# A fused attention and two-MLP kernel on Trainium2: where in a step GpSimd issues its half of the relayout

## The chip, the cores and the metric

The kernel runs on 1 core of one Trainium2 chip. The metric is the device time of one execution in microseconds; the kernel before was run three times: 644.7, 645.08 and 647.82 us, median 645.08 us.

## The reference, cut to what matters

Attention with two mixings of the heads (one before and one behind the softmax), followed by two MLPs. Batch 2, 12 heads, 448 positions, head width 64; 896 tokens of width 768; both MLPs have 2048 hidden units. Everything is float32.

```python
scores = scale * np.matmul(q, k.transpose(0, 1, 3, 2))
scores = np.einsum('bhij,hg->bgij', scores, w_pre)
scores = scores - np.max(scores, axis=-1, keepdims=True)
attn = np.exp(scores)
attn = attn / (np.sum(attn, axis=-1, keepdims=True) + 1e-09)
attn = np.einsum('bhij,hg->bgij', attn, w_post)
return np.matmul(attn, v).astype(np.float32)
...
x = attn_out.transpose(0, 2, 1, 3).reshape(B * S, H * D)
x = elu(x @ moe_w_in) @ moe_w_out
return silu(x @ moe2_w_in) @ moe2_w_out
```

## The kernel before, in words

**Attention** (about the first third of the span). The scores come out of TensorE with query positions on the partitions: `qk_pair` (line 149) makes them for a tile T of 128 query rows and a pair of heads, and ScalarE and VectorE copy them to the SBUF tile `s` (`smap[T]`, lines 156 and 158). The mixing over heads needs heads on the partitions. So the **relayout**, a DMA from SBUF to SBUF, brings the scores of 10 query positions with all 12 heads, 120 rows of 448 floats, into the buffer `blk` (`move`, line 168). There are 45 such blocks for each batch, 90 in all.

The work goes on in **45 steps of two blocks each**, c = 0 and c = 1. `blk` has 3 slots (`NBUF`), and step s uses slot s % 3. In `step(s)`:

- `premix(s)` (line 198) multiplies both blocks by w_pre on TensorE: 8 matmuls, first the four of c = 0, then the four of c = 1.
- In steps 8, 10, 12 and so on, `av_pair` (line 269, 32 matmuls) multiplies finished attention rows by v. In steps 0 to 6, 11 to 16 and 17 to 34 `qk_pair` makes new scores (8 matmuls a step).
- `postmix(s - 1)` (line 241, 56 matmuls) applies w_post to the block pair of the step before.
- `rmax(s)` (VectorE, line 204), `exps(s)` (ScalarE, line 216, with the sums) and `recip(s)` make the softmax. `recip` has two small VectorE instructions (lines 224 and 225) and then two GpSimd instructions (line 229) that multiply w_post by 1/sum: this is the **softmax factor** `krn`, which `postmix(s)` reads in the next step.
- ScalarE and VectorE empty the PSUM banks: `qk_evac` (lines 156, 158), `post_evac` (lines 133, 135), `av_evac` (line 280). In a step without `av_pair`, `recip(s)` stands behind these in the program.
- `relayout(s + AHEAD)` with `AHEAD = 2` issues the DMAs for two steps later, and `run(D_AT, s)` issues loads from HBM.

The order is written out by hand, and each engine takes its instructions in the program's order; semaphores let an engine wait for another. A relayout into slot (s + 2) % 3 needs the slot that `premix(s - 1)` reads, and the rows of `smap` that it copies.

**Queues.** The relayout of c = 0, with the pieces that `early` puts a step ahead, goes through SP's queue, which also carries most loads from HBM. For steps 3 to 31 (`POOLED = (3, 32)`) the relayout of c = 1 is issued by GpSimd: 35 DMAs for 29 blocks, since some blocks come in two or three pieces. The relayouts for steps 0 to 2 and from step 32 on are on SP for both c. On GpSimd in a step stand, in this order: the two `krn` instructions of step s, the DMA for c = 1 of step s + 2, and in some later steps (from step 30 on) parts of the conversion of x for the first MLP (`split_x`, lines 391 and 392).

**The MLPs** (from about 206 us to the end) are rows of matmuls with weights that are loaded and split in time. The change does not touch them.

Of the kernel before, what the change touches and what calls it, by code (L numbers as in the profile page):

```python
# [18 lines left out]
B, H, S, D = 2, 12, 448, 64  # L19
# [11 lines left out]
NBUF = 3  # L31
NE = 3
LEAD = 5
POOLED = (3, 32)
# [3 lines left out]
AHEAD = 2  # L38
# [41 lines left out]
def attn_moe_moe(ctx: ExitStack, tc: tile.TileContext, q, k, v, w_pre, w_post, w1i, w1o, w2i, w2o, out):  # L80
    nc = tc.nc
# [24 lines left out]
    blkb = ap_.tile([P, NBUF, 2, S], F32, name="blk")  # L106
# [30 lines left out]
    smap = {}  # L137
# [14 lines left out]
    def qk_evac(e):  # L152
        for T, p, pq in sev:
            o = smap[T][:, 2 * p + e]
            if e == 0:
                nc.scalar.activation(o, pq[0], AF.Copy, scale=0.125)  # L156
            else:
                nc.vector.tensor_scalar(o, pq[1], 0.125, None, op0=ALU.mult)
        if e == 1:
            sev.clear()  # L160

    seq = [(b, n) for b in range(B) for n in range(KB)]
    NB = len(seq) // 2

    def move(s, c, piece):
        T, r, d, m, i = piece
        eng = nc.gpsimd if c and POOLED[0] <= s < POOLED[1] else nc.sync
        eng.dma_start(blkb[4 + H * i:4 + H * (i + m), s % NBUF, c], smap[T][r:r + d * (m - 1) + 1:d])

    def early(n):  # L170
        x = BLOCKS[seq[n]]
        return [y for y in x if n % 2 == 0 and y[0] < x[-1][0]]

    def relayout(s):

        if s >= NB:
            return
        for c in range(2):
            gone = early(2 * s + c)
            for piece in BLOCKS[seq[2 * s + c]]:  # L180
                if piece not in gone:
                    move(s, c, piece)
        if s + 1 < NB:
            for piece in early(2 * s + 2):
                move(s + 1, 0, piece)

# [5 lines left out]
    def premix(s):  # L192
        tags = (("pre1", "pre2"), ("av", "pre0"), ("qk1", "pre0"))[s % 2 + (s % 2 and s > NB - 9)]
        pre[s] = [ps.tile([P, S], F32, name=f"pre{s}_{r}", tag=tags[r], bufs=1) for r in range(2)]
        for c in range(2):
            for r in range(2):
                o = slice(HS * r, HS * r + (HS if r == 0 else BW))
                nc.tensor.matmul(pre[s][r][HS * c:HS * c + HS], kpre[o], blkb[o, s % NBUF, c], start=True, stop=True, tile_position=(HS * r, HS * c))  # L198

    def rmax(s):  # L200
        n = prow(s)
        nmx[s] = ap_.tile([P, 2], F32, name=f"nmx{s}", tag="nmx", bufs=3)
        for r in range(2):
            nc.vector.tensor_reduce(nmx[s][:n, r:r + 1], pre[s][r][:n], axis=AX.X, op=ALU.max, negate=True)  # L204
            if r == 0 and s - 1 in LATE:
                recip(s - 1)

    def exps(s, between=None):
        n = prow(s)
        pexp[s] = []  # L210
        sums[s] = ap_.tile([P, 2], F32, name=f"sum{s}", tag="sum", bufs=3)
        for r in range(2):
            if r and between:
                between()
            t = ap_.tile([P, S], F32, name=f"pe{s}_{r}", tag="pe", bufs=4)
            nc.scalar.activation(t[:n], pre[s][r][:n], AF.Exp, bias=nmx[s][:n, r:r + 1], scale=1.0, accum_out=sums[s][:n, r:r + 1])  # L216
            pexp[s].append(t)
        del pre[s], nmx[s]

    def recip(s):  # L220

        n = prow(s)
        z = sums.pop(s)
        nc.vector.tensor_scalar(z[:n], z[:n], 1e-9, None, op0=ALU.add)
        nc.vector.reciprocal(z[:n], z[:n])  # L225
        kr[s] = []
        for r in range(2):
            t = ap_.tile([P, H, 5], F32, name=f"krn{s}_{r}", tag="krn", bufs=4)
            nc.gpsimd.tensor_scalar(t[:n], kps[:n], z[:n, r:r + 1], None, op0=ALU.mult)  # L229
            kr[s].append(t)  # L230
# [3 lines left out]
    def postmix(s):  # L234

        w = pst[s] = [x.rearrange("p (r c) -> p r c", r=2) for x in pbank]
        for r, m in [(0, m) for m in range(6)] + [(0, 6), (1, 6)] + [(1, m) for m in range(6)]:
            u, j = r if m == 6 else m % 2, m // 2
            for c in range(2):
                o = slice(HS * c, HS * c + BW)  # L240
                nc.tensor.matmul(w[c][HS * u:HS * u + HS, r, j * BW:(j + 1) * BW], pexp[s][r][o, m * HS:(m + 1) * HS], kr[s][r][o].rearrange("p h i -> p (h i)"), start=True, stop=True, tile_position=(HS * c, HS * u))  # L241
        del pexp[s], kr[s]
# [4 lines left out]
    def post_evac(s):  # L247
        for c, w in enumerate(pst.pop(s)):
            b, n = seq[2 * s + c]
            T, n = 4 * b + n // 12, n % 12  # L250
            if T not in amap:
                amap[T] = ap_.tile([P, 4 * H, TI], F32, name=f"a{T}", tag="a", bufs=2)
            o = amap[T][:NV, :, n * BI:(n + 1) * BI].rearrange("p x (r i) -> p r x i", r=2)
            evac((nc.scalar, nc.vector)[c], o, w[:NV].rearrange("p r (x i) -> p r x i", i=5))
# [18 lines left out]
    def av_evac():  # L273
        for T, p, m, av in xev:
            b, t = tiles[T]
            if b not in xmap:
                xmap[b] = cp.tile([P, NP, S], F32, name=f"xr{b}", tag=f"xr{b}")
                if b == 1:
                    cp.tile([P, 40], F32, name="align3")
            nc.scalar.copy(xmap[b][:, p:p + 2, t * TI:t * TI + m], av[:, :, :m])  # L280
        xev.clear()

    def av_split():
        for T, p, m, av in xsp:
            c = slice(tiles[T][1] * TI, tiles[T][1] * TI + m)
            x = x1_tile()
            nc.scalar.copy(x[:, p:p + 2, 0, c], av[:, :, :m])
            nc.scalar.copy(xmap[1][:, p:p + 2, c], av[:, :, :m])
            nc.vector.tensor_tensor(x[:, p:p + 2, 1, c], av[:, :, :m], x[:, p:p + 2, 0, c], op=ALU.subtract)
        xsp.clear()  # L290
# [24 lines left out]
    for s in range(AHEAD):  # L315
        relayout(s)
# [8 lines left out]
    def at(d, step, f):  # L325
        d.setdefault(int(step), []).append(f)
# [20 lines left out]
    def run(d, s):  # L347
        for f in d.get(s, []):
            f()

    def step(s):
        if s < NB:
            premix(s)
        if s - 1 in LATE:
            rmax(s)
        run(X_AT, s)
        run(QK_AT, s)
        run(F_AT, s)
        if 0 <= s - 1 < NB:
            postmix(s - 1)  # L360
        if s < NB:
            if s - 1 not in LATE:
                rmax(s)
            exps(s, (lambda: post_evac(s - 1)) if s in TURN else None)
        two = s in X_AT
        if two:
            run(B_AT, s)
            if s < NB:
                recip(s)
            av_evac()  # L370
            av_split()
            run(A_AT, s)
        qk_evac(0)
        qk_evac(1)
        if 0 <= s - 1 < NB and s not in TURN:
            post_evac(s - 1)
        if not two:
            run(B_AT, s)
            if s < NB and s not in LATE:
                recip(s)  # L380
        relayout(s + AHEAD)
        run(D_AT, s)
        run(M_AT, s)
# [63 lines left out]
    def ring(n):  # L447
        if n >= O2:
            n += 2 * sum(x[0] == "out" and x[3][0] == KS and i % 2 == 1 for i, x in enumerate(chunks[O2:n]))
        return n % (NE + 1)  # L450
# [169 lines left out]
    for s in range(NB + 1):  # L620
        step(s)
        if s == NB - 2:
            cm_s2.__exit__(None, None, None)
            cm_s1.__exit__(None, None, None)
            cm_ws, mo["ws"] = pool("wst", bufs=1, side="right")
            load_w(NE)
            load_w(NE + 1)
# [369 lines left out]
    for t, n_ in zip(x, "B11_0 B11_1 B11_2 T1_0 T1_1 T1_2 B21_0 B21_1 B22_0 T2_0 T2_1 B22_1 T3_0 T3_1 T4_0 T4_1 B21_2 T2_2 T3_2 T4_2 B22_2".split()):  # L997
        a, i = n_.split("_")
        xt[1][a, int(i)] = t
    for n in range(O1 + 8, I2):  # L1000
# [4 lines left out]
        if po:  # L1005
            c = chunks[n][2]
# [122 lines left out]
    while n < NCH:  # L1129
        c, k = chunks[n][2:]  # L1130
# [4 lines left out]
        i = n - O2  # L1135
        xs = made[i] if i < len(made) else []
        nx = [x[3][0] == KS for x in chunks[n + 1:n + 3]]
        d = [(ring(n + 1) + i) % 4 for i in range(4)]
# [87 lines left out]
```

## Time and profile before

| | |
|---|---|
| three runs, median | 645.08 us (644.7 to 647.82) |
| profiled execution, its own time | 647.85 us |
| its span, from the first to the last instruction | 646.0 us |
| TensorE busy | 612.0 us (95%) |
| VectorE busy | 453.6 us (70%) |
| ScalarE busy | 374.0 us (58%) |
| GpSimd busy | 83.4 us (13%) |
| mean granted TensorE clock | 0.984 |
| chain that ended last, by share | TensorE 79%, DMA 9%, VectorE 4%, ScalarE 3%, GpSimd 2% |

The profile shows one execution. An engine is busy while it executes; waiting on semaphores and issuing DMAs on SP's or ScalarE's queue do not count. "PE" is TensorE's matmuls, "PEld" its weight loads, "DVE" VectorE, "ACT" ScalarE, "POOL" GpSimd, "SP" the queue engine. The chain of waits is found by going back from the last instruction, at each step to what released it. Within a window, the chain is the one that ended last in that window.

### The profile page before, as it was taken

To read this page: it belongs to the slowest core of one execution; us is meant where nothing else is said; L and a number is where in the kernel's file an instruction comes from. 1 tells how busy PE (TensorE), PEld (TensorE's weight loads), DVE (VectorE), ACT (ScalarE), POOL (GpSimd) and SP (SyncE) were. 2 spreads that over 40 slices of the span, in tenths; PEclk is the share of its full clock that TensorE was granted. 3 is DMA by queue.
4 is the path that set the end of the run, shared out by engine and by line. 5 is a ranking of instruction groups with operands and counts; after the bars stand their busy time and mean duration, and the time that the engine had idled before them with its cause. 6 is when DMAs were issued, how large, how long until landed. Compare 5 with 4: busy or idle time off the path is not lost.

```text
span 646.0 us, 15007 instructions
## 1 busy us (share of the span) xinstructions
PE 612.0 (95%) x6139; PEld 515.9 (80%) x6139; DVE 453.6 (70%) x755; ACT 374.0 (58%) x686; POOL 83.4 (13%) x152
## 2 busy tenths in 40 slices
PE   9758989877999999999999999999999999999997
PEld 3435545545667998999999999999999999999996
DVE  5634656655885579988677667559988879976642
ACT  4534656645786487675787454337677675543321
POOL 1322432414456300000000000000000000000000
PEclk9878999989899999999999999999999999999999
DMA  6543555645344132442324422434424332443601
GB/s 232 179 130 124 156 176 147 158 130 171 121 163 127 50 98 97 150 145 82 123 92 129 139 89 82 147 98 146 148 98 148 109 104 82 138 148 129 204 34 57
DMA packets 36385, 82.04 MB, mean 127 GB/s; under 512 B 5197, under 2 KB 15845, under 8 KB 36317
## 3 DMA queue, kind: packets, MB, share of 16 engines
q1 hardware_dynamic: 31549, 70.63, 34.0%
q0 software_dynamic: 2608, 6.25, 3.3%
q10 hardware_dynamic: 2160, 4.21, 2.2%
q8 instruction: 48, 0.79, 0.5%
q14 instruction: 20, 0.16, 0.1%
HBM read 59.05 MB, written 2.75 MB: 96 GB/s over the span
## 4 chain that ended last, share of the span: by engine, by line
PE 79%; DMA 9%; DVE 4%; ACT 3%; POOL 2%; issue 1%; POOLq 0%; SPq 0%; DVEq 0%; ACTq 0%
PE po L552 29%; PE b L815 26%; DMA blk<-s 9%; PE pre L198 4%; PE q L1075 3%; PE post L241 3%; PE pq L149 3%; PE ph L538 3%; PE av L269 3%; PE po L1075 2%; DVE nmx L204 2%; POOL krn L229 2%; ACT pe L216 2%; PE post L538 1%; PE warm L309 1%
## 5 line engine op out<-in xcount | busy, mean ns | idle before, releaser
L216 ACT ACTIVATE pe<-pre,nmx 124x448 f32<-124x448 f32 x90 | 56.4, 631 | 68.4 <-DVE nmx L204 63.4
L815 PE MATMUL b<-x,we 128*128 128x448 f32 x360 | 93.8, 363 | 0.0
L198 PE MATMUL pre<-blk,kpre 64*64 64x448 f32 (+1 forms) x360 | 67.9, 577 | 27.2 <-DMA blk<-s 27.2
L204 DVE TENSOR_REDUCE nmx<-pre 124x1 f32<-124x448 f32 x90 | 52.0, 615 | 44.7 <-PE pre L198 40.3
L815 PEld LDWEIGHTS b<-x,we 128*128 128x128 f32 x360 | 67.5, 188 | 4.7 <-DVE we L558 0.2
L241 PEld LDWEIGHTS post<-krn,pe 60*64 60x64 f32 x2520 | 54.1, 142 | 20.4 <-issue 11.8
L815 PE MATMUL b<-rr,we 128*128 128x448 f32 x288 | 69.5, 362 | 0.0
L767 ACT ACTIVATE wr<-wr 128x768 f32<-128x768 f32 (+1 forms) x61 | 52.9, 868 | 17.7 <-DMA wr<-in_w1o_dram 8.2
L552 PE MATMUL po<-ge,we 128*128 128x448 f32 x216 | 60.3, 362 | 0.0
L552 PE MATMUL po<-gs,we 128*128 128x448 f32 x216 | 59.9, 362 | 0.0
L763 DVE SCALAR_TENSOR_TENSOR wc<-wr,wc 128x768 int32<-128x768 int32 (+1 forms) x62 | 56.2, 907 | 4.0 <-ACT wr L767 0.4
L815 PEld LDWEIGHTS b<-rr,we 128*128 128x128 f32 x288 | 54.1, 188 | 3.5
L241 PE MATMUL post<-krn,pe 60*64 60x60 f32 x2520 | 55.4, 229 | 1.1 <-POOL krn L229 0.9
L229 POOL TENSOR_SCALAR krn<-kps,sum 124x60 f32<-124x60 f32 x90 | 38.2, 432 | 129.9 <-DVE sum L225 90.7
L149 PE MATMUL pq<-kt,qt 64*64 64x448 f32 x336 | 51.7, 579 | 0.8 <-ACT s L156 0.8
L198 PEld LDWEIGHTS pre<-blk,kpre 64*64 64x64 f32 (+1 forms) x360 | 17.0, 142 | 42.7 <-DMA blk<-s 40.0
L552 PE MATMUL po<-x,we 128*128 128x448 f32 x192 | 50.1, 362 | 0.0
L269 PEld LDWEIGHTS av<-a,v 128*64 128x64 f32 x768 | 36.9, 137 | 16.3 <-ACT a L133 5.7
L509 DVE TENSOR_TENSOR we<-wc,we 128x640 fp32r<-128x640 f32 (+1 forms) x31 | 26.7, 862 | 30.2 <-ACT we L500 30.1
L552 PE MATMUL po<-ta,we 128*128 128x448 f32 x168 | 44.8, 362 | 0.0
L552 PEld LDWEIGHTS po<-ge,we 128*128 128x128 f32 x216 | 40.5, 188 | 2.7
L552 PEld LDWEIGHTS po<-gs,we 128*128 128x128 f32 x216 | 40.5, 188 | 2.7
(155 smaller groups left out, 1132.8 us busy)
## 6 DMA issues: line engine op xcount, KB each, us to landing
wr<-in_w2i_dram SPq DMA_DIRECT2D x32, 384.0 KB
wr<-in_w1i_dram SPq DMA_DIRECT2D x29, 384.0 KB
blk<-s SPq DMA_DIRECT2D x53, 210.0 KB
wr<-in_w1o_dram SPq DMA_DIRECT2D x24, 384.0 KB
wr<-in_w2o_dram SPq DMA_DIRECT2D x24, 384.0 KB
blk<-s POOLq DMA_DIRECT2D x24, 210.0 KB, 4.0
wr<-in_w1o_dram SPq DMA_DIRECT2D x12, 256.0 KB
wr<-in_w2o_dram SPq DMA_DIRECT2D x12, 256.0 KB
```

What stands on the lines that cost most here:

```text
L149: nc.tensor.matmul(pq[e][HS * c:HS * c + HS], qT[T][half, p, HS * c:HS * c + HS], kT[p][half, bs[c % len(bs)]], start=True, stop=True, til ...
L198: nc.tensor.matmul(pre[s][r][HS * c:HS * c + HS], kpre[o], blkb[o, s % NBUF, c], start=True, stop=True, tile_position=(HS * r, HS * c))
L204: nc.vector.tensor_reduce(nmx[s][:n, r:r + 1], pre[s][r][:n], axis=AX.X, op=ALU.max, negate=True)
L216: nc.scalar.activation(t[:n], pre[s][r][:n], AF.Exp, bias=nmx[s][:n, r:r + 1], scale=1.0, accum_out=sums[s][:n, r:r + 1])
L229: nc.gpsimd.tensor_scalar(t[:n], kps[:n], z[:n, r:r + 1], None, op0=ALU.mult)
L241: nc.tensor.matmul(w[c][HS * u:HS * u + HS, r, j * BW:(j + 1) * BW], pexp[s][r][o, m * HS:(m + 1) * HS], kr[s][r][o].rearrange("p h i -> p ...
L269: nc.tensor.matmul(avt[T][e * D:(e + 1) * D, p % 2, :m], vall[b][:NV, h, j], amap[T][:NV, j * H + h, :m], start=j == 0, stop=j == 3, tile_ ...
L552: nc.tensor.matmul(po, wt[:, kk * P:(kk + 1) * P], g_op(moe, k0 + kk, hf, gi), start=(k0 == 0 and n_ == 0), stop=(k0 + kn == (KF, KS)[moe] ...
L763: nc.vector.scalar_tensor_tensor(cc, r[:, :, 1], 3, cc, op0=ALU.logical_shift_left, op1=ALU.bitwise_or)
L767: nc.scalar.activation(hf, hf, AF.Prelu, scale=2.0 ** -112, alpha=2.0 ** 32)
L815: nc.tensor.matmul(o, wt[:, u * KH + i * P:u * KH + (i + 1) * P], X[x, i][:, xi], start=start and n_ == 0, stop=n_ == 8, skip_group_check= ...
L1075: nc.tensor.matmul(o, wt[:, u * KH + i * P:u * KH + (i + 1) * P], t[i][:, xi] if x == "B22" else t[:, i, xi], start=start and n_ == 0, sto ...
```

## The change

The relayout of c = 1 by GpSimd for step s + 2 was issued at the end of step s, behind that step's `recip(s)`. It is now issued as the first thing of step s, in front of `premix(s)`; on GpSimd it so stands in front of the two `krn` instructions of step s and behind those of step s - 1. `relayout` is called twice in a step: with `pool=True` at the beginning, for the blocks that GpSimd moves, and at the old place for all others. Which blocks GpSimd moves, the pieces, the buffers and the order on SP stay as they were.

```diff
     def move(s, c, piece):
         T, r, d, m, i = piece
-        eng = nc.gpsimd if c and POOLED[0] <= s < POOLED[1] else nc.sync
-        eng.dma_start(blkb[4 + H * i:4 + H * (i + m), s % NBUF, c], smap[T][r:r + d * (m - 1) + 1:d])
+        (nc.gpsimd if pooled(s, c) else nc.sync).dma_start(blkb[4 + H * i:4 + H * (i + m), s % NBUF, c], smap[T][r:r + d * (m - 1) + 1:d])
+
+    def pooled(s, c):
+        return c == 1 and POOLED[0] <= s < POOLED[1]
...
-    def relayout(s):
+    def relayout(s, pool=False):
 
         if s >= NB:
             return
         for c in range(2):
+            if pooled(s, c) != pool:
+                continue
             gone = early(2 * s + c)
             for piece in BLOCKS[seq[2 * s + c]]:
                 if piece not in gone:
                     move(s, c, piece)
-        if s + 1 < NB:
+        if s + 1 < NB and not pool:
             for piece in early(2 * s + 2):
                 move(s + 1, 0, piece)
...
     def step(s):
+        relayout(s + AHEAD, True)
         if s < NB:
             premix(s)
```

## Rows read from the trace of the kernel before

**Rows 1.** Page, parts 1 and 2: busy time; the clock in 40 slices.

```profile
PE 612.0 (95%) x6139; PEld 515.9 (80%) x6139; DVE 453.6 (70%) x755; ACT 374.0 (58%) x686; POOL 83.4 (13%) x152
...
PEclk9878999989899999999999999999999999999999
```

**Rows 2.** Groups by line, window 21.7:168.8: busy, mean ns | idle before.

```profile
L198 PE MATMUL pre<-blk,kpre 64*64 64x448 f32 x240 | 51.8, 594 | 27.2 <-DMA blk<-s 27.2
...
L229 POOL TENSOR_SCALAR krn<-kps,sum 124x60 f32<-124x60 f32 x62 | 25.9, 424 | 99.1 <-DVE sum L225 79.5 <-ACT a L133 16.5 <-ACT xr L280 2.2
```

**Rows 3.** Chain of waits, windows 16:46, 64:98, 160:178: start, us, what.

```profile
21.15 3.86 DMA blk<-s
...
25.05 0.94 PE pre L198 x2
...
31.27 5.70 DMA blk<-s
...
37.01 1.24 PE pre L198 x2
...
43.95 5.43 DMA blk<-s
...
78.57 4.79 DMA blk<-s
...
83.40 0.59 PE pre L198 x2
...
91.05 4.97 DMA blk<-s
...
160.39 0.77 PE pre L198 x2
```

**Rows 4.** The same chain, windows 160:178 and 182:206.

```profile
165.48 1.79 PE av L269 x32
...
169.00 0.76 PE pre L198 x8
...
172.08 1.79 PE av L269 x32
...
175.59 0.85 PE pre L198 x8
...
198.53 0.77 PE pre L198 x8
```

**Rows 5.** Line 168: GpSimd's issues (ns min/median/max), and issue to landing.

```profile
L168 POOL DMA_DIRECT2D blk<-s x35: 538/645/842, 21.1 to 156.4; - x35
...
DMA to landing us min/median/max: 2.6/4.3/6.2
```

**Rows 6.** Timeline of GpSimd: start us, us, what, xcount [idle before].

```profile
17.48 0.84 POOL L229 TENSOR_SCALAR krn<-kps,sum 124x60 f32<-124x60 f32 x2 [14.42 <-ACT s L156]
...
87.96 0.65 POOL L168 DMA_DIRECT2D blk<-s  x1
89.62 0.83 POOL L229 TENSOR_SCALAR krn<-kps,sum 124x60 f32<-124x60 f32 x2 [1.02 <-DVE sum L225]
90.41 1.19 POOL L168 DMA_DIRECT2D blk<-s  x2
...
123.37 1.78 POOL L168 DMA_DIRECT2D blk<-s  x3
```

**Rows 7.** Timeline from 80.4 to 83.9 us: VectorE, GpSimd, SP.

```profile
80.89 0.69 DVE L135 COPY a<-post 128x480 f32<-128x480 f32 x1
81.01 0.65 POOL L168 DMA_DIRECT2D blk<-s  x1
81.58 0.81 SPq L168 DMA_DIRECT2D blk<-s  x1
```

**Rows 8.** Windows: busy (x) of PE, PEld, DVE, ACT, POOL; PEclk, DMA, GB/s.

```profile
21.70:64.30 42.60, 30.31 (x622) 19.20 (x614) 19.05 (x47) 18.43 (x49) 12.35 (x26) 0.84 0.42 130
64.30:168.80 104.50, 89.44 (x1988) 55.50 (x1983) 63.39 (x146) 60.17 (x153) 35.53 (x73) 0.97 0.51 152
```

## The prediction

> **What bounds the kernel now.** I read the page first, then the attention stretch by groups, then its chain of waits, then GpSimd's timeline. On the page TensorE is busy 95% of the span [rows 1], and the MLPs behind 206 us keep it so. The slices of its clock dip only in the first 160 us [rows 1], in the attention steps that the change touches. There the groups by line show TensorE idle for 27.2 us in front of `premix`, all of it put down to the DMA into `blk` [rows 2]. The chain of waits says which DMA: the one that GpSimd issues. The chain runs from a `krn` to the DMA issued behind it, from there to the third and fourth pair of matmuls of a `premix` (those of c = 1), through the softmax of that step to the next `krn`, and to the next DMA. In the stretch from 78 to 96 us one turn is 83.40 - 78.57 = 4.8 us of DMA and then the softmax [rows 3]. The DMA issued behind `krn(s)` is for step s + 2, so **a turn of this loop spans two steps**, and the steps come in pairs: an odd step waits for its c = 1, the even one follows closely, the next odd one waits again.
>
> The pace: step 3 begins its c = 1 matmuls at 25.05 us and step 31 at 160.39 us [rows 3], so 28 steps take 135.3 us, 9.67 us a pair. Behind the last relayout from GpSimd the chain is TensorE alone: from one `av_pair` to the next 172.08 - 165.48 = 6.60 us for a pair of steps with scores and `av` [rows 4]. Without new scores it is (198.53 - 175.59) / 4 = 5.74 us, over eight steps from 35 to 43 [rows 4]. So about 3 us of each pair is the loop's.
>
> **What moves.** All 35 issues of GpSimd [rows 5], for 29 blocks, go in front of the two `krn` of their step. No instruction and no byte is added. On GpSimd's queue the order `krn(s)`, DMA, `krn(s+1)`, DMA stays; what changes is that the DMA behind `krn(s)` is now for step s + 3 instead of s + 2. Nothing on SP's queue is passed: its c = 0 pieces, early pieces and loads keep their order. `split_x` on GpSimd comes in steps from 30 on and is not passed either, since the last moved issue is in step 29.
>
> **Does the issue wait for something else in its new place?** It needs the slot that `premix(s-1)` read; `krn(s-1)`, right in front of it on GpSimd, is computed from that same `premix`, so the slot is free. It needs its rows of `smap`: these are copied at least a step before, in one case (step 25, in step 23) in step 22, by copies that stand beside `krn(22)`. If it waits there, `krn(23)` and through it `postmix(23)` are behind it, but these come a step later. I cost it at nothing; the cover is GpSimd's idle time, 99.1 us in front of `krn` in this stretch [rows 2].
>
> **The issue itself** takes 0.54 to 0.84 us [rows 5], and now stands in front of `krn(s)`. In the old order the DMA of the step before stood there too. Nothing is added.
>
> **The new loop.** A turn now spans three steps. From the c = 1 matmuls to the next issue it is 87.96 - 83.40 = 4.56 us [rows 3, 6], from issue to landing 4.3 us (median; 2.6 to 6.2) [rows 5]: 8.9 us for three steps, or 5.9 us a pair. That is under TensorE's 6.6 us for a pair with scores and `av`. The margin is thin, though: three steps at 6.6 us a pair are 9.9 us, and pairs are uneven. The longest landing, 6.2 us, makes 10.8 us, or 7.2 us a pair.
>
> Here a rule of the Trainium skill can be laid beside the row. The page "DMA: Bandwidth & Descriptors", section "Anatomy of one DMA — SWDGE (gpsimd) path", fits a DMA issued by GpSimd as 2.0 us plus its bytes over 436e3 a microsecond, which for 210 KB is 2.5 us. The trace doesn't agree: its smallest is 2.6 us and its median 4.3 us [rows 5]. By this formula of the Trainium skill the loop would be 7.1 us for three steps, TensorE would bound everywhere, and the sum below would come out at its floor, a gain of 51 us.
>
> **The sum**, from the first wait to step 33, whose `premix` starts at 169.00 us [rows 4], 15 pairs:
> - Start: the DMA for step 3 is issued behind `krn(0)`, which ends at 17.48 + 0.84 = 18.3 us [rows 6], not at 21.15; with the same 3.86 us it lands at 22.2 us instead of 25.0 [rows 3].
> - Steps 3 to 10, four pairs, with scores or `av` but not both. Floor 5.8 us, from the 5.74 above. The loop there is slower: matmul to issue 31.27 - 25.05 = 6.2 and 43.95 - 37.01 = 6.9 us, landing 5.70 and 5.43 us [rows 3], together 12 us, or 8.0 us a pair, while the clock granted was 0.84 [rows 8]. With fewer idle stretches I expect the clock nearer 1, as in the later window (0.97) [rows 8]. I take the middle of 8.0 and the 5.9 of the full-clock loop, 7.0: 28.0 us.
> - Steps 11 to 32, eleven pairs with both: 6.6 us by TensorE, and 0.2 us as an estimate for landings over the median: 6.8 x 11 = 74.8 us. Bounds 6.6 and 7.2.
>
> Step 33 then starts at 22.2 + 28.0 + 74.8 = 125.0 us instead of 169.0. **Gain 44 us.** Everything behind it moves up unchanged: there SP issues both relayouts already, and the work of weights is tied to steps. The profiled execution (647.85 us, of which 646.0 us span) becomes 603.9 us; it is 2.8 us above the median of the runs, so against 645.08 us I predict **601 us**. Floor of the terms: 22.2 + 4 x 5.8 + 11 x 6.6 = 118.0, gain 51, 594 us. Upper bounds: 22.2 + 4 x 8.0 + 11 x 7.2 = 133.4, gain 36, 609 us.
>
> **What is late next**: where a step has scores and `av`, TensorE; in steps 3 to 10 the softmax of VectorE and ScalarE; then the c = 0 transfers.
>
> **The rivals.**
> 1. *The transfers get in each other's way.* The same bytes go in about two thirds of the time, so the DMA share of 0.42 and 0.51 [rows 8] rises to about 0.6 and 0.75. Loads from HBM stand in SP's queue in front of c = 0 pieces; in 12 of the steps from 1 to 30 `run(D_AT, s)` issues one. If each made one `premix` 1 to 2 us late (an estimate from the spread of the landings, 6.2 - 4.3 us), 12 to 24 us of the gain would go: 613 to 625 us. For it: landings reach 6.2 us already. Against: c = 0 is issued as soon as `premix` three steps back has read its slot, and none of the waits on the chain that I followed is for it.
> 2. *GpSimd's issues are starved by VectorE.* If an issue took several times as long beside a VectorE copy, say the 4.3 us of a landing, GpSimd would need 2 x (0.84 + 4.3) = 10.3 us a pair, more than the 9.67 of now: 22.2 + 15 x 10.3 = 176.7 us, and the kernel would be **slower**, 653 us. It decides from an issue of 4.0 us on (9.67 / 2 - 0.84). The same price holds if GpSimd must hold an issue until its last transfer has landed. Against both: an issue at 81.01 us beside a copy from 80.89 to 81.58 took 0.65 us [rows 7]; two issues in 1.19 us at 90.41 us began while the one of 87.96 us could hardly have landed, and three followed each other in 1.78 us [rows 6].
>    The Trainium skill has this as a trap, page "SBUF — State Buffer", section "SBUF: two separate sides": VectorE's copies within SBUF lock GpSimd out and its descriptors wait, with 3.1 us in place of 0.62. By that figure a pair would be 2 x (0.84 + 3.1) = 7.9 us, and the time about 617 us; the copies here read PSUM, and the row above shows no such price.
> 3. *It does nothing*: the issue waits in its new place for the slot or for a copy, and starts no sooner. 645 us. Against it stands the argument on the slot above.
>
> **How the numbers follow.** Chances: forecast 0.75 (594 to 609 us), rival 1 0.18 (609 to 625), rival 2 0.04, rival 3 0.03. A difference of 0.5%, 3.2 us, is about what a measurement of this kernel can tell from no change. Faster by more: 0.93; within: 0.03; slower: 0.04. The range takes in the forecast and half of rival 1: 594 to 618 us.
>
> **What would show it.** In the profile after: the first issue of line 168 on GpSimd at about 18.3 us instead of 21.1; idle time of `premix` for `blk` under 8 us instead of 27.2; step 33's `premix` at about 125 us; chain in steps 11 to 32 mostly TensorE; clock of the early slices near 1; issues still 0.5 to 0.9 us. Wrong would be: landings over 6 us throughout, `premix` waiting for c = 0 from SP, or a pace of over 7.2 us a pair.

## The result and the profile after

The changed kernel is **faster**: ratio of its runs to those of the kernel before 0.9487, 95% interval 0.9422 to 0.9552, some 33 us. The medians are 612.59 us and 644.89 us. The profiled execution took 610.48 us (span 608.7 us) against 647.85 us (span 646.0 us), 37 us less; it was the shortest of the changed kernel's runs, that of before the longest of its own at that time. Single runs over 1.5% longer than the fastest of their kernel (of the changed kernel the one of 628.52 us) are left out of the ratios; where such a run was the profiled one (e7 and e9), its extra time lies behind step 33, 490 us against 477 in the changed kernel. The prediction was 601 us, range 594 to 618.

The page of the changed kernel, busy time and clock, then the group of `premix` over the whole span (code lines have moved by some lines: 198 is now 202, 229 is 233, 168 is 167):

```profile
PE 592.4 (97%) x6139; PEld 505.3 (83%) x6139; DVE 452.6 (74%) x755; ACT 373.0 (61%) x686; POOL 83.9 (14%) x152
...
PEclk9999999999999999999999999999999999999999
...
L202 PE MATMUL pre<-blk,kpre 64*64 64x448 f32 x360 | 50.3, 542 | 8.2 <-DMA blk<-s 8.0
```

The wait for `blk` in front of `premix` fell from 27.2 us [rows 2] to 8.0 us, and the dips of the clock in the first 160 us [rows 1] are gone. TensorE's busy time fell by 20 us (612.0 to 592.4) with the same 6139 matmuls. Part of that is the clock that TensorE gets back once it idles less: a matmul of `premix` took 594 ns in the mean of the attention stretch [rows 2] and takes 542 now. It is not all: 12.4 of the 20 us fell behind 64.3 us, where the granted clock was 0.97 already (89.44 us [rows 8] against 77.03 in the window from 50.20 us, shown further below). A second cost shows under "Which steps wait": a `premix` whose c = 1 comes late keeps TensorE busy about twice as long, besides the wait. How the rest divides is not worked out here.

The chain of waits of the changed kernel from 14 us on: start us, us, what.

```profile
18.84 6.17 DMA blk<-s
...
25.05 0.59 PE pre L202 x2
...
29.61 5.97 DMA blk<-s
...
49.27 6.31 DMA blk<-s
...
78.26 6.55 DMA blk<-s
...
108.61 5.71 DMA blk<-s
...
131.68 0.76 PE pre L202 x8
...
168.32 1.40 PE ph L543 x6
```

Where the old chain had a DMA in each pair of steps [rows 3], there are five into `blk` now. Step 33's `premix` starts at 131.68 us instead of 169.00 [rows 4]. From there to the first matmul of the first MLP outside the steps it is 168.32 - 131.68 = 36.64 us; in the kernel before that matmul stands at

```profile
205.60 1.43 PE ph L538 x6
```

so 205.60 - 169.00 = 36.60 us. What follows lasts 440.4 us in both (646.0 - 205.6 and 608.7 - 168.3). The whole gain of the profiled executions, 37.3 us, is made in front of step 33.

### The profile page after: what moved, and what is told of

It reads as the page before. It is cut to its first block, busy times and chain, and to the rows that moved or that the text cites. A ratio compares the mean times of both kernels' runs of the same rounds, so it can differ in the third digit from the quotient of the medians.

```text
span 608.7 us, 15033 instructions
## 1 busy us (share of the span) xinstructions
PE 592.4 (97%) x6139; PEld 505.3 (83%) x6139; DVE 452.6 (74%) x755; ACT 373.0 (61%) x686; POOL 83.9 (14%) x152
## 4 chain that ended last, share of the span: by engine, by line
PE 87%; DMA 6%; DVE 3%; ACT 3%; issue 1%; POOL 1%; DVEq 0%; ACTq 0%; POOLq 0%
PE po L557 31%; PE b L820 28%; PE av L273 5%; DMA blk<-s 5%; PE pre L202 4%; PE pq L149 4%; PE post L245 4%; PE q L1080 4%; PE ph L543 3%; PE po L1080 2%; DVE nmx L208 1%; PE post L543 1%; ACT pe L220 1%; POOL krn L233 1%; PE warm L313 1%
## 5 line engine op out<-in xcount | busy, mean ns | idle before, releaser
L245 PEld LDWEIGHTS post<-krn,pe 60*64 60x64 f32 x2520 | 45.5, 135 | 21.6 <-issue 10.3
L202 PE MATMUL pre<-blk,kpre 64*64 64x448 f32 x360 | 50.3, 542 | 8.2 <-DMA blk<-s 8.0
L245 PE MATMUL post<-krn,pe 60*64 60x60 f32 x2520 | 47.1, 219 | 2.0 <-POOL krn L233 1.7
L149 PE MATMUL pq<-kt,qt 64*64 64x448 f32 x336 | 42.1, 562 | 1.0 <-ACT s L156 1.0
L752 ACT CAST we<-wc 128x768 fp32r<-128x768 f32 (+1 forms) x34 | 28.2, 830 | 22.4 <-DVE wc L768 8.9
```

What stands on the lines that cost most here:

```text
L149: nc.tensor.matmul(pq[e][HS * c:HS * c + HS], qT[T][half, p, HS * c:HS * c + HS], kT[p][half, bs[c % len(bs)]], start=True, stop=True, til ...
```

## The experiments

They are variants of the changed kernel; "steps 11 to 33" is the time from step 11's `premix` to step 33's in the profile, 81.5 us in the changed kernel (50.15 to 131.68 us).

**e1: only the transfers for odd steps are moved.**

```diff
-        relayout(s + AHEAD, True)
+        if (s + AHEAD) % 2 == 1:
+            relayout(s + AHEAD, True)
...
+        if (s + AHEAD) % 2 != 1:
+            relayout(s + AHEAD, True)
         relayout(s + AHEAD)
```

> Only the GpSimd relayouts for odd steps are issued at the beginning of the step; those for even steps stay behind the softmax factor. Theory (a turn of the loop krn - DMA - premix - softmax bounds the pace, and whichever parity is still tied over two steps sets it): the even steps now carry the two-step loop, 4.56 + 4.3 = 8.9 us a pair, so step 33's premix starts near 22.2 + 15 x 8.9 = 156 us and the time is about 632 us (625 to 640). Rival (only odd steps ever wait, since the trace of before shows waits of odd steps alone; even ones follow for free): nearly the whole gain, 610 to 615 us.

Measured: 634.47 us, ratio 0.9798 (0.9758 to 0.9837). The chain of waits now shows the loop in the even steps:

```profile
87.21 0.83 POOL krn L233 x2
88.04 0.43 POOL blk L167
...
88.62 5.30 DMA blk<-s
93.96 0.96 PE pre L202 x2
...
156.18 0.76 PE pre L202 x8
```

The `krn` is that of step 16, the `premix` that of step 18. Step 33 starts at 156.18 us, where 156 was expected. That even steps hardly waited in the kernel before was no sign of slack: they were carried by the wait of the odd ones.

**e2: only the transfers for even steps are moved** (the same edit with the parities exchanged).

> Only the GpSimd relayouts for even steps are issued at the beginning of the step. Theory: the odd steps keep the two-step loop of the kernel before, so nothing is gained: 640 to 648 us. Rival (each early issue gives back its own share): about half the gain, near 628 us.

Measured: 651.54 us, ratio 1.0078 (1.0051 to 1.0106): no gain, and a loss of 5 us that the theory did not have; the interval leaves it over 1. Chain and landings:

```profile
79.36 4.93 DMA blk<-s
...
84.34 0.59 PE pre L202 x2
...
89.56 7.36 DMA blk<-s
...
96.97 1.13 PE pre L202 x4
```

```profile
DMA to landing us min/median/max: 3.2/4.8/7.4
```

GpSimd now issues the odd step's transfer and the next even one's back to back, and the landing is 4.8 us in the median instead of 4.3 [rows 5]. The odd steps still wait for it. That the longer landings make the loss fits, but is not shown. The shares of the parities don't add up (2% faster, 0.8% slower, together 5.1% faster): it is one loop, and both parities must leave it.

**e3: issue as soon as the slot is free.** GpSimd issues for step s + 3 right behind `premix(s)`, in front of that step's `krn`, so that the softmax is no longer in the loop.

```diff
...
+    def ready(n, s):
+        return s >= 0 and n < NB and all(QK_END[y[0]] < s for y in BLOCKS[seq[2 * n + 1]])
...
-        relayout(s + AHEAD, True)
+        if not ready(s + AHEAD, s - 1):
+            relayout(s + AHEAD, True)
         if s < NB:
             premix(s)
+        if ready(s + NBUF, s):
+            relayout(s + NBUF, True)
```

`QK_END[T]` is the step in which the scores of tile T are completed.

> GpSimd issues the relayout for step s + 3 right behind premix(s), in front of that step's krn, as soon as the slot is free (in two steps, where the scores are made too late for that, at the place of the changed kernel). That takes the softmax out of the loop. Theory (what is left of the waits in the changed kernel is landings of about 6 us that the three-step loop with the softmax in it cannot cover): waits for blk in front of premix nearly vanish, pairs with scores and av take 6.6 us, step 33's premix starts at 119 to 122 us instead of 131.7, time 598 to 603 us. Rival (the rest of the waits is c = 0 from SP, or bandwidth): no more than 3 us faster than the changed kernel, 608 to 613 us.

**e4: all relayouts on SP's queue.**

```diff
-POOLED = (3, 32)
+POOLED = (0, 0)
```

> All relayouts on SP's queue, none on GpSimd. Theory (the loss in the kernel before came from GpSimd's order of work, the DMA standing behind a krn that depends on the softmax, not from the transfers): SP is not tied to the softmax, so its issues go out when the slot is free, and the time is at or below that of the changed kernel, 598 to 612 us. Rival (SP's queue with the loads from HBM in it delays them, which is why GpSimd was used): 618 us or more.

Measured on one chip: e3 602.94 us, ratio 0.9327 (0.9294 to 0.936); e4 602.83 us, ratio 0.932 (0.9286 to 0.9353). Both beat both kernels. Two rows of e3, the group of `premix` and the landings:

```profile
L202 PE MATMUL pre<-blk,kpre 64*64 64x448 f32 x360 | 47.1, 542 | 2.0 <-DMA blk<-s 1.0 <-issue 0.7 <-ACT xr L284 0.2
```

```profile
DMA to landing us min/median/max: 3.0/5.3/8.2
```

The landings are longer than in the changed kernel (5.3 us against 4.4 in the median), and yet TensorE waits 1.0 us for `blk` instead of 8.0, and that for a transfer of SP's; no matmul waits for one of GpSimd's. So it is not the length of a landing by itself that costs, but what stands in the loop with it. Step 33 starts at 124.01 us in e3 and at 124.69 us in e4, not at 119 to 122. The rest is no wait for `blk`, as e3's window of steps 11 to 33 shows (columns as in [rows 8]):

```profile
47.92:124.01 76.09, 74.33 (x1972) 50.27 (x1976) 62.35 (x146) 59.58 (x153) 34.10 (x70) 1.00 0.73 209
```

TensorE is busy for 74.33 of the 76.09 us, about what eleven pairs of 6.6 us and one more `av_pair` of 1.8 us in step 23 make (74.4), and the other 1.76 us are a single stop that waits for nothing in the trace (last section).

The Trainium skill, page "DMA: Bandwidth & Descriptors", section "Issuing engines are not separate DMA queues", says that DMAs issued by different engines run on the same 16 engines and that spreading them saves only the time to issue. e3 and e4 fit that, at 602.9 and 602.8 us. GpSimd as the issuer was worth nothing by itself here; what its queue added was an order, the DMA behind a `krn`.

**e5: the changed kernel again**, beside the next two.

> The changed kernel once more, beside the next two on one chip. Both theories: a ratio of 0.942 to 0.956 to the kernel before, 608 to 616 us.

Measured: ratio 0.9524 (0.9436 to 0.9611); steps 11 to 33 take 132.97 - 51.56 = 81.4 us. What follows is about the 8 us of waits that are left.

**e6 and e8: fewer loads from HBM beside the transfers.** e6 (cut ahead of this: the matmuls read the first batch's k and v):

```diff
...
-    for T, st in ((3, 7), (4, 15), (5, 20)):
-        at(D_AT, st, lambda T=T: load_q(T))
-    at(A_AT, 26, lambda: load_q(6, nc.scalar))
+    for T in range(3, 7):
+        qT[T] = qT[T - 3]
...
-        at(e, st, lambda p=p, e=e: load_k(1, p, nc.scalar if e is A_AT else nc.sync))
+        pass
...
-        at(e, st, lambda g=g, e=e: load_v(1, g, nc.scalar if e is A_AT else nc.sync))
+        pass
```

> The changed kernel without the loads of q, k and v that are issued from step 7 on (the tiles loaded before are read again, so the second batch is computed with the first one's k and v and old q). Theory (the landings of about 6 us that the three-step loop does not cover come from loads from HBM that are under way at the same time): no landing over 5.2 us from step 9 on, apart from steps in which weights are loaded; steps 11 to 33 take 74 to 77 us instead of 81.5, time 4 to 7 us below e5. Rival (the relayout's own transfers, or GpSimd's issuing, make the landings long): landings and time within 2 us of e5.

e8 leaves out the later k and v as e6 does, keeps the rotation of the q buffers and loads one pair of heads of six:

```diff
...
-        at(D_AT, st, lambda T=T: load_q(T))
-    at(A_AT, 26, lambda: load_q(6, nc.scalar))
+        at(D_AT, st, lambda T=T: load_q(T, parts=(slice(0, 1),)))
+    at(A_AT, 26, lambda: load_q(6, nc.scalar, (slice(0, 1),)))
...
```

> The changed kernel without the later loads of k and v and with a sixth of the later loads of q, but with the rotation of the q buffers as it was (in e6 that rotation had shifted, and ScalarE waited 2.5 us for scores at line 501). It computes with the first batch's k and v and with one pair of heads of q for all. Theory (loads under way make the landings long, and the three-step loop passes that on): steps 11 to 33 take 75 to 78 us, against 81.5 in the changed kernel; the span is 4 to 6 us shorter. Rival (loads don't matter): 80 us or more.

Measured: e6 ratio 0.95 (0.9414 to 0.9586), steps 11 to 33 129.56 - 50.20 = 79.4 us; e8 ratio 0.9445 (0.9393 to 0.9496), span 605.8 us, steps 11 to 33 128.70 - 49.17 = 79.5 us. The intervals can't tell either from the changed kernel; the stretch is 2 us shorter in both, which is less than either theory had and not quite nothing. The chain of e8:

```profile
18.48 5.45 DMA blk<-s
...
28.55 6.05 DMA blk<-s
...
68.46 6.18 DMA blk<-s
...
83.56 6.55 DMA blk<-s
...
128.70 0.76 PE pre L202 x8
```

Landings fall to 3.9 us in the median, and the wait of step 12 (from 49.27 us in the changed kernel) has left the chain, but steps 6, 18 and 22 still wait for landings over 6 us. In the last, issued at 83.56 us, hardly a load was under way; SP had issued four pieces of relayout from 79.95 us on.

**e7: the first loads of v later.**

```diff
-    for g, st in enumerate((0, 1, 3, 5)):
+    for g, st in enumerate((3, 4, 5, 6)):
```

> The changed kernel with the four loads of v for the first batch issued in steps 3, 4, 5 and 6 instead of 0, 1, 3 and 5 (first use in step 8). Theory (the 6.17 us landing for step 3, in place of 3.86, came from two of these loads in front of it): that landing falls to 4.5 us or less and step 3 starts its c = 1 about 2 us sooner; the loads then lie beside the transfers for steps 5 to 8, which gives part of it back: 0 to 3 us below e5. Rival: the landing stays over 5.5 us, and the time is that of e5.

Measured: ratio 0.9559 (0.9495 to 0.9623), 612.9 to 613.4 us in three of its four runs; nothing gained. The profiled execution is the fourth, of 625 us. Its first landings: 2.7 us for step 3, as the theory had it, and 9.3 us for step 6, issued at 27.47 us among the four loads of v (24.17, 25.46, 27.08 and 29.87 us on SP). A delay taken out of one landing was put into another.

**e9: e3 with the small loads of e8.**

> The same loads left out of the kernel that issues when the slot is free (e3). Theory (there the loop has slack for landings of 6 to 8 us): the loads matter little, 0 to 2 us less than e3's 601.0 us span. Rival (loads cost something other than the landings, such as time of the issuing engines): the same 4 to 6 us as between the changed kernel and e8.

Measured: 601.55 us, ratio 0.9339 (0.9285 to 0.9394), not to be told from e3's 0.9327. The saving of 4 to 6 us that the rival wanted does not show. In the profile steps 11 to 33 take 121.78 - 47.27 = 74.5 us, about TensorE's own time of 74.4 above, and e3's stop of 1.76 us is not there.

**e10 and e11: without the relayouts of c = 0** from step 3 on; e11 has the small loads of e8 as well.

```diff
         T, r, d, m, i = piece
+        if c == 0 and s >= NBUF:
+            return
```

> The changed kernel without the relayouts of c = 0 from step 3 on (its blocks of c = 0 are mixed from old rows); all loads stay. Theory (what makes GpSimd's landings long is all that is under way beside them: the loads, and also the c = 0 relayouts of SP): with c = 0 gone the landings fall to 3.5 us in the median and reach 5 us only beside a load; steps 11 to 33 take 74 to 77 us against 81.5. Rival (c = 0 does not matter for them, or the waits that are left are for c = 0 itself, then also gone, but with landings as before): landings keep a median over 4 us and a longest over 6.

> Both left out: the c = 0 relayouts from step 3 on, and the later loads as in e8. Theory: landings of 2.5 to 3.5 us nearly everywhere from step 8 on, waits for blk only in the first steps, steps 11 to 33 at TensorE's floor, 73 to 74.5 us. Rival (a third cause, in GpSimd's own issuing): single landings over 5 us stay.

Measured: e10 ratio 0.9413 (0.9349 to 0.9476), e11 0.9367 (0.9279 to 0.9455); steps 11 to 33 take 131.50 - 51.36 = 80.1 us and 129.29 - 51.45 = 77.8 us. Landings of e10, then of e11:

```profile
DMA to landing us min/median/max: 2.5/3.5/8.3
```

```profile
DMA to landing us min/median/max: 2.4/3.5/7.8
```

The median falls to 3.5 us, so the other transfers do lengthen GpSimd's. But behind the first steps single landings over 5 us stay (in e10 for steps 12, 18, 28 and 29, in e11 for 18 and 28), and both stretches miss what was expected. In e11 the two are the only waits in the chain from step 11 on, and beside each goes out a load of 384 KB of weights for the first MLP, which no run left out. The chain, then ScalarE's and SP's queue:

```profile
70.87 5.36 DMA blk<-s
...
106.61 5.32 DMA blk<-s
```

```profile
70.74 0.33 ACTq L451 DMA_DIRECT2D wr<-in_w1i_dram  x1
...
107.11 0.33 SPq L451 DMA_DIRECT2D wr<-in_w1i_dram  x1
```

Traffic explains a part of the long landings; for the others the loads of weights stand untested, and the rival's third cause, in GpSimd's own issuing, is not shown.

**Which steps wait.** Behind step 3 all the waits in the changed kernel's chain are for even steps: 6, 12, 20 and 28. The reason is in the timeline of GpSimd and of `premix` on TensorE: start us, us, what, xcount, idle before.

```profile
64.69 0.65 POOL L167 DMA_DIRECT2D blk<-s  x1
...
67.15 0.65 POOL L167 DMA_DIRECT2D blk<-s  x1
...
78.26 0.64 POOL L167 DMA_DIRECT2D blk<-s  x1
```

```profile
52.54 0.56 PE L202 MATMUL pre<-blk,kpre 64*64 64x448 f32 x2
...
69.03 1.31 PE L202 MATMUL pre<-blk,kpre 64*64 64x448 f32 x8
73.68 0.94 PE L202 MATMUL pre<-blk,kpre 64*64 64x448 f32 x8
...
82.60 0.93 PE L202 MATMUL pre<-blk,kpre 64*64 64x448 f32 x4
84.86 0.97 PE L202 MATMUL pre<-blk,kpre 64*64 64x448 f32 x4 [1.33 <-DMA blk<-s]
...
112.45 0.93 PE L202 MATMUL pre<-blk,kpre 64*64 64x448 f32 x4
```

The transfers are those for steps 16, 17 and 20, the matmuls those of the same steps and of steps 12 and 28. An even step's `premix` comes 82.60 - 78.26 = 4.3 us behind its issue, the odd step's 73.68 - 67.15 = 6.5 us, and c = 1 is wanted about 0.4 us later. So the landing for step 20 may take 4.7 us, that for step 17 6.9. A landing of 6.55 us is late for step 20 and would not be for step 17. These two numbers do not hold for every step. Worked out the same way for steps 11 to 31, the four shortest covers are all of even steps, 3.7 us (step 12: 52.54 - 49.27 + 0.4), 4.2 (step 28: 112.45 - 108.61 + 0.4) and 4.7 (16 and 20); the others, of either parity, run from 5.1 to 9.2 us. Of the four only step 16's landing, 4.6 us, was in time.

The lines also show what a late c = 1 costs besides the wait. Eight matmuls of a `premix` take 0.94 us when both blocks are there (73.68). At step 20 the four of c = 0 take 0.93 us alone, and the four of c = 1 another 0.97 us behind the wait of 1.33: TensorE is busy for about 1 us more.

**e12: only the even steps' transfers when the slot is free.** The edit is to e3:

```diff
-        return s >= 0 and n < NB and all(
+        return n % 2 == 0 and s >= 0 and n < NB and all(
```

> Only the relayouts for even steps are issued when the slot is free (as in e3); those for odd steps stay at the changed kernel's place. Theory (pairs are uneven: an even step's transfer is issued behind krn of an odd step and wanted some 4.5 us later, an odd step's some 6.5 us later; so of the transfers behind step 3 only the even steps' ones are late, whatever makes them 5 to 6.6 us long): the waits at steps 6, 12, 20 and 28 go, steps 11 to 33 take 74 to 77 us, and the time is within 3 us of e3's 602.9: 600 to 606. Rival (long landings hurt both parities, so only half of what e3 gains over the changed kernel comes): 606 to 610.

Measured: ratio 0.9428 (0.9351 to 0.9504). Three runs are 604.8, 606.97 and 610.29 us, so two of them lie in the rival's range and one in the theory's, and the time decides neither way. The profile says more. Group of `premix`, and what is left of DMA behind step 3 in the chain:

```profile
L202 PE MATMUL pre<-blk,kpre 64*64 64x448 f32 (+1 forms) x360 | 48.2, 549 | 3.0 <-DMA blk<-s 2.6 <-issue 0.3
```

```profile
45.73 7.09 DMA blk<-s
...
127.42 0.76 PE pre L202 x8
```

The waits of steps 6, 20 and 28 are gone; that of step 12 is not, since its two pieces stand on GpSimd behind the transfer for step 11, which still waits for its `krn`, and then took 7.09 us. Steps 11 to 33 take 127.42 - 49.07 = 78.4 us, a little over half of the way from 81.5 down to e3's 76.1 (124.01 - 47.92); that misses the 74 to 77 us of the theory and includes a stop of 1.99 us (last section). That no odd step waits in this chain is for the theory.

## Why the prediction was right, and where its sizes were off

**Right: what bounds the kernel.** That GpSimd's DMA stood in a loop with the softmax, that a turn spanned two steps and now spans three, is shown from three sides: moving the odd steps' transfers alone leaves the even steps in the loop at the pace that was worked out (e1), moving the even steps' alone gains nothing (e2), and taking the softmax out of the loop nearly ends the waits although landings get longer (e3, e4).

**Right but for 0.3 us: nothing new waits on GpSimd.** The issue costs what it did; the moved issues and their landings, and one issue from GpSimd's timeline:

```profile
L167 POOL DMA_DIRECT2D blk<-s x35: 538/642/842, 18.8 to 119.6; - x35
...
DMA to landing us min/median/max: 2.6/4.4/6.6
...
49.27 1.28 POOL L167 DMA_DIRECT2D blk<-s  x2 [0.34 <-PE av L273]
```

I had named one step in which the issue would find its scores just being copied (25). There is another, step 19, whose issue waits 0.6 us for a copy of ScalarE at 74.58 us; it costs nothing on the chain, as was said of the other. The issue for step 12 goes out 0.34 us late, put down to an `av_pair`, and this one is on the chain. Rival 2, issues starved beside VectorE, and rival 3, no earlier start, have nothing in the trace. (Rival 2's second price, 7.9 us a pair, put 3.1 us, the time of a whole transfer, in the place of an issue's; the longest issue here takes 0.84 us.)

**The sum, term by term**, in the profiled execution:

- *Start*, 22.2 us predicted, 25.05 measured. I took the 3.86 us landing of the kernel before for an issue that goes out 2.3 us sooner. It took 6.17 us. The transfer now lies beside the first loads of v; e7, which moves these, shows 2.7 us for it. The issue was earlier and the landing was not.
- *Steps 3 to 10*, 28.0 us predicted, 50.15 - 25.05 = 25.1 measured. The slow-clock loop of 8.0 us a pair, half of my mean, did not return: the clock is 1.00 throughout, as the windows show (columns as in [rows 8]).

```profile
21.70:50.20 28.50, 23.37 (x666) 14.23 (x657) 19.20 (x48) 18.86 (x52) 13.20 (x28) 1.00 0.63 196
50.20:131.70 81.50, 77.03 (x1972) 50.77 (x1976) 62.74 (x146) 59.39 (x153) 34.87 (x72) 1.00 0.67 196
```

- *Steps 11 to 32*, 74.8 us predicted, 81.5 measured. **This is the term that was mis-sized.** "0.2 us as an estimate for landings over the median" made 2.2 us for eleven pairs. The chain has three waits into `blk` in this stretch, at landings of 6.31, 6.55 and 5.71 us, and about 7 us are lost there against pairs of 6.6 us: 81.50 - 77.03 = 4.5 us in which TensorE idles, nearly all of it in front of these three, and about 1 us more of busy time at each. I had written that pairs are uneven and then divided the loop evenly, 8.9 us against 9.9. The four shortest covers, all of even steps, are 3.7 to 4.7 us for landings with a median of 4.4, and three of the four came late. Besides, step 23 has an `av_pair` of its own between those of 22 and 24, which the words on the kernel before leave out too, so that eleven times 6.6 us left out one of twelve groups, 1.8 us by [rows 4].

The first two cancel by chance, and the third makes step 33 start at 131.7 instead of 125.0 us: 37.3 us of gain in place of 44.

**Luck in the range.** The range of 594 to 618 us holds the result, but not by the forecast's own bounds, 594 to 609: 612.59 us lies in the half of rival 1 that the range took in, 609 to 625 us at a chance of 0.18, and it came there for another reason than that rival's. One of the named signs of being wrong came as well: in steps 11 to 32 the pace is 81.5 / 11 = 7.4 us a pair, over the bound of 7.2 (7.25 without step 23's `av_pair`). That bound took the longest landing in a loop divided evenly over its steps.

**Rival 1** named the transfers in each other's way, with the c = 0 pieces in SP's queue as the late ones. Half of it came true. The DMA share rose to 0.63 and 0.67, as expected, and with other transfers left out the landings are shorter (e8, e10, e11). But the transfers that came late were GpSimd's own, for even steps, and no load of q, k and v or c = 0 taken out gave back more than 4 us of the stretch (81.5 to 77.8 with both).

**The rule of the Trainium skill** that was weighed, 2.0 us plus bytes over the bandwidth ("DMA: Bandwidth & Descriptors", "Anatomy of one DMA — SWDGE (gpsimd) path"), is met by the smallest landings of 210 KB, 2.5 to 2.6 us (2.6 in the changed kernel, 2.5 in e10 and e11); the median of the changed kernel, 4.4 us, is far over it, and the floor of 594 us that followed from it was not reached by any of the kernels. Nor do the landings go by the bytes; issues of the changed kernel by size, the last number the median landing in us:

```profile
blk<-s POOLq DMA_DIRECT2D x24, 210.0 KB, 4.5
...
blk<-s POOLq DMA_DIRECT2D x4, 21.0 KB, 3.7
```

A tenth of the bytes lands 0.8 us sooner; in the kernel before it is 4.8 us for 21 KB and 4.0 for 210.

**Left open:** what makes single landings of 5 to 6 us with the loads of q, k and v and c = 0 left out (e11), and what stops TensorE for 1.76 us in e3.

## What to carry to other kernels

A transfer issued from the queue of an engine that also computes inherits all that this engine waits for; put the issue at the place where its buffer comes free, or on a queue with no such work. Count over how many steps a loop of issue, landing and compute turns, and when steps are uneven count the cover for each kind of step: the shortest one sets the waits, not the mean. An operand that never waits in the trace may be carried by one that does, so a fix of the waiting one alone can move the wait instead of ending it.

## What was not expected

In e3, with the wait for `blk` nearly gone, TensorE stood still for 1.8 us in the middle of the 56 matmuls of a `postmix`, all of which wait for the same `krn`; the trace names no releaser. e12 has the same at the same step. TensorE's timeline in e3, then in e12:

```profile
78.36 0.51 PE L245 MATMUL post<-krn,pe 60*64 60x60 f32 x20 [1.76 <-issue]
```

```profile
81.53 0.51 PE L245 MATMUL post<-krn,pe 60*64 60x60 f32 x20 [1.99 <-issue]
```

A window of e12 just in front of its stop (columns as in [rows 8]):

```profile
76.00:79.50 3.50, 3.50 (x109) 2.33 (x102) 2.78 (x7) 2.20 (x5) 2.06 (x4) 1.00 0.92 254
```

The DMA engines are 92% busy there (95% in e3 from 73.00 to 76.60 us), against 0.67 for the stretch of steps 11 to 33 in the changed kernel. The trace also has a DMA queue of kind "instruction", with a packet of 16 KB mostly every 4 to 6 us. In e3 there is none between 68.44 and 75.79 us and in e12 none between 71.73 and 79.02; TensorE stops 0.8 and 0.5 us behind the start of the packet that then comes, and goes on 1.4 and 1.3 us behind its end. e9, which is e3 with fewer loads, has no such stop there; gaps as long before 31 us, in e3 and in the changed kernel, have no stop over 0.7 us behind them. That the busy engines hold up TensorE's instructions would fit, but no run tests it.
